# Two layers of cached attention and a token mixer on one core: half of the kv heads stay away from the changes of layer, and their weights' place goes to V

## The chip, the cores and the metric

The kernel runs on one core of one Trainium2 chip. Its time is the device time of one execution in microseconds (us). A profiled execution gives in addition the span from the first to the last instruction and what every engine and every DMA queue did in it.

The engines are named as in the profile: PE multiplies matrices (PEld is its loading of the stationary operand), DVE, ACT and POOL work element by element, and SP here does nothing but issue DMAs, in the order in which the program lists them. An SP instruction that has to wait holds up all loads behind it.

## The reference, cut to what matters

Two identical layers run on `x` of 2 batch rows (b) by 512 channels, one token each. A layer is attention over a cache, then a mixer, each added to its input:

```python
x = x + _A_ref(_layernorm(x), A_k_cache, A_v_cache, A_wq, A_wo)
x = x + _B_ref(_layernorm(x), B_w1, B_b1, B_w2, B_b2)
# the same two lines once more

def _A_ref(x, k_cache, v_cache, wq, wo):       # 32 q heads, 8 kv heads, 32768 cached rows of 128
    q = x @ wq                                  # 4 q heads share one kv head
    p = softmax(q . k * 128 ** -0.5)
    return (p @ v) @ wo

def _B_ref(x, w1, b1, w2, b2):                  # hidden size F = 1792
    h = layernorm(x)
    return gelu(h * w1[f] + b1[f]) summed over f with w2[f], + b2
```

Everything is float32. The caches K and V of one batch row and one kv head are 16.8 MB each, and both layers read the same caches. With 2 rows and 8 heads that is 268 MB for K and 268 MB for V in each layer, and as much again in the second. The weights `wq` and `wo` of one kv head together are 2.1 MB.

## The kernel before, in words

**Units, chunks and slots.** A unit is one (layer, b, h): one kv head of one batch row in one layer. There are 32. A unit's K and its V are cut into 8 chunks (NCH) of 4096 cached rows each: 128 partitions by 16 KB, 2.1 MB. The list `units` gives the order of the units. Slot s handles K chunk s and V chunk s - 10 of that long row of 256 chunks, because V runs one unit and LAG = 2 slots behind K. The main loop (lines 666 to 684) does for each slot: issue the load of K (`load_k`), `k_chunk` on PE, the small steps listed in `pre`, issue the load of V (`load_v`), `v_chunk` on PE, the steps listed in `post`. In slots for which `paired(s)` holds (PAIRED, line 21) two chunks are loaded by one DMA: 32 KB a partition, 4.2 MB. Before the change these are slots 0 to 47 and 212 on.

**PE's work in a slot.** `k_chunk` is 8 matmuls (16 in the records) of scores (line 263); `v_chunk` is 8 matmuls into `acc` (line 353). Per unit there are further: `make_q` (lines 221 and 233) shortly before its first slot, the maximum and the sum of the softmax, `out_1` (line 398, gathers `acc`) in `pre` at the slot in which the next unit's first V chunk is handled, and `out_2` (line 411, times `wo`) in `post` of that slot. After the last unit of a (layer, b) the mixer runs over some ten slots (`mix_1` to `mix_4`, `hidden_tile`, `hidden_out`); its result is needed by `make_q` of that row in the next layer.

**The change of layer.** A layer's first units for row 0 need the mixer's output for row 0. So three units (BRIDGE) of row 1 stand between the last unit (0, 0, h) and the first unit (1, 0, h), and the same holds on the other side for row 1. Layer 1 begins with head 7 (`turned`), which is the last of layer 0, so that V of (0, b, 7) can in part stay in the memory for (1, b, 7).

**The memory.** One tile `mem` of 54,784 floats in each partition (214 KB) holds all of it:

- from 0 to 12,287 the ring: 3 cells of 4096 floats (16 KB) for K and V chunks in turn. Its buffers follow a fixed list, PLACES. In paired slots the ring is 6 cells long, as 3 pairs, and takes part of what comes next, which is then not in use.
- then `kept`, 9728 floats: the parts of V of (0, b, 7) that stay. KEPT says how many of a chunk's 8 quads (a quad is 512 floats a partition, 0.262 MB) stay: 19 of 64 quads. `load_v` loads them in layer 0 and leaves them out in layer 1, for either row.
- then the weights of all 8 heads, 4096 floats each. `load_weights(h)` (line 88) runs once for every head, in `post` six slots ahead of the head's first unit, on SP like all large loads.

A load into a cell waits until PE has read what lay there. With three cells, the load of K chunk s waits for `v_chunk` of slot s - 2, and the load of V in slot s for `k_chunk` of slot s - 1.

**The end.** The last V chunks come in one DMA per piece (PIECES). When the last has come: `v_chunk` multiplies the last 8 row blocks one by one (line 365), `out_1` copies `acc` half on DVE and half on ACT (`halves_copy`, lines 387 and 388) and gathers it by 4 matmuls (line 398), and `last_mixer` multiplies by `wo` with the result spread over all partitions (line 506, 8 matmuls one after the other), takes the statistics (line 514 and on), and does the 14 hidden tiles: the first three by ACT alone (DIRECT, line 546), the others in groups (TAIL_GROUPS) for which DVE does the affine part (line 553) and ACT the gelu (line 557), with PE (line 536) adding them up. Line 563 and the store of line 564 end the program.

Of the kernel before, what the change touches and what calls it, by code (L numbers as in the profile page):

```python
# [8 lines left out]
F32 = mybir.dt.float32  # L9
AF = mybir.ActivationFunctionType  # L10
ALU = mybir.AluOpType
# [6 lines left out]
SUB = 2  # L18
PACK = 4
RING = 3  # L20
PAIRED = ((0, 48), (212, 1 << 30))
LAG = 2
KEPT = {0: 8, 2: 4, 4: 4, 6: 3}
BRIDGE = 3
PIECES = (32, 16, 8, 4, 4)
THIN = 8
QT = 4
DIRECT = 3
TAIL_GROUPS = (3, 3, 4, 1)
EPS = 1e-5  # L30


@with_exitstack
def gqa_mixer_kernel(ctx: ExitStack, tc: tile.TileContext, x, kt, v, wqo, cols, out):

# [35 lines left out]
    nc.scalar.dma_start(xcols, x)  # L73


    W = wqo.shape[2] // 2
    RING0 = 0
    KEPT0 = RING0 + RING * CK
    kept_columns = sum(KEPT.values()) * QT * DH
    order = [HKV - 1] + list(range(HKV - 1))  # L80
    home = {h: KEPT0 + kept_columns + k * 2 * W for k, h in enumerate(order)}
    mem = const.tile([P, KEPT0 + kept_columns + HKV * 2 * W], F32, name="mem")
    kept = mem[:, KEPT0 : KEPT0 + kept_columns]
    wq_sb = [mem[:, home[h] : home[h] + W].rearrange("p (t c) -> p t c", t=DT) for h in range(HKV)]
    wo_sb = [mem[:, home[h] + W : home[h] + 2 * W].rearrange("p (t c) -> p t c", t=R) for h in range(HKV)]

    def load_weights(h):
        nc.sync.dma_start(mem[:, home[h] : home[h] + 2 * W], wqo[h])


    def places(base, k, size):
        return [base + (j % RING) * size for j in range(k, k + RING)]

    PLACES = (
        (PAIRED[0][0], [], places(RING0, 0, 2 * CK)),
        (PAIRED[0][1], [RING0 + j * CK for j in (2, 3, 4)], places(RING0, 0, CK)),
        (PAIRED[1][0], [], places(RING0, 2, 2 * CK)),
    )
    turn = {}

    def buffer(s, size):
        k = max(j for j in range(len(PLACES)) if PLACES[j][0] <= s)
        _, ahead, loop = PLACES[k]
        i = turn.get(k, 0)
        turn[k] = i + 1
        f = ahead[i] if i < len(ahead) else loop[(i - len(ahead)) % len(loop)]
        return mem[:, f : f + size]

    def paired(s):
        return any(a <= s < b for a, b in PAIRED)  # L110

    load_weights(0)
    cols_sb = const.tile([P, 3 * FT + 1], F32, name="cols_sb")
# [15 lines left out]
    nc.vector.tensor_reduce(  # L129
        selg, ident.rearrange("p (g r) -> p r g", g=NG)[:, : R * QT, :], axis=AX.X, op=ALU.add  # L130
    )

    sel1 = selg[:, 0:1].to_broadcast([P, P])
    qpad = [const.tile([P, 64], F32, name=f"qpad{k}") for k in range(2)]
# [13 lines left out]
    def first_input():  # L148
# [19 lines left out]
            xnT[0, b] = const.tile([P, DT], F32, name=f"xnT_0_{b}")  # L168
            nc.vector.tensor_scalar_mul(xnT[0, b], cen[:, b, :], rs[:, b : b + 1])

    heads = list(range(HKV))
    turned = heads[-1:] + heads[:-1]
    lay = {(layer, b): [(layer, b, h) for h in (turned if layer else heads)] for layer in range(LAYERS) for b in range(B)}
    units = (
        lay[0, 0]
        + lay[0, 1][:BRIDGE]
        + lay[1, 0][:-BRIDGE]
        + lay[0, 1][BRIDGE:]
        + lay[1, 0][-BRIDGE:]
        + lay[1, 1]  # L180
    )
    assert len(units) == NU and B == 2

    xT, xnT = {}, {}

    def row_tile():

        return S[HALVES - 1]
# [17 lines left out]
    def unit_of(n):  # L206

        return units[n]

    q_ps = {}  # L210

# [30 lines left out]
    def load_k(s):  # L242
        n, c = divmod(s, NCH)
        layer, b, h = unit_of(n)
        m = 2 if paired(s) else 1
        t = buffer(s, m * CK)
        f0 = (c % 2) * CK
        nc.sync.dma_start(t, kt[b * HKV + h, c // 2, :, f0 : f0 + m * CK])
        for j in range(m):
            k_at[n, c + j] = t[:, j * CK : (j + 1) * CK]  # L250
# [67 lines left out]
    def load_v(s):  # L318
        n, c = divmod(s - NCH - LAG, NCH)
        layer, b, h = unit_of(n)  # L320
        u = b * HKV + h
        m = 2 if paired(s) else 1
        w = QT * DH
        f0 = (c % 2) * CK
        stay = stays(n, c)
        if stay and layer == 0:
            nc.sync.dma_start(kept[:, place[c] : place[c] + stay * w], v[u, c // 2, :, f0 : f0 + stay * w])
        if stay == JT // QT:
            return
        t = buffer(s, m * CK)  # L330
        k0 = stay * QT
        for k in PIECES if s + m == NU * NCH + NCH + LAG else (m * JT - k0,):
            nc.sync.dma_start(t[:, k0 * DH : (k0 + k) * DH], v[u, c // 2, :, f0 + k0 * DH : f0 + (k0 + k) * DH])
            k0 += k
        for j in range(m):
            v_at[n, c + j] = t[:, j * CK : (j + 1) * CK]

    def v_chunk(n, c):
        w = QT * DH
        very_last = n == NU - 1 and c == NCH - 1  # L340
        stay = stays(n, c)
        if stay:
            own = kept[:, place[c] : place[c] + stay * w]
        vc = v_at.pop((n, c), None)
        half, i = divmod(c, PACK)


        a, c2 = divmod(i, PACK // 2)
        quads = JT // QT - (THIN // QT if very_last else 0)
        for q in range(quads):  # L350
            g = q % NG
            col = (c2 * (JT // QT) + q) * 32 + a * R * QT
            nc.tensor.matmul(  # L353
                acc[32 * g : 32 * g + R * QT, :],
                S[half][:, col : col + R * QT],
                (own if q < stay else vc)[:, q * w : (q + 1) * w],
                start=(c == 0 and q < NG),
                stop=(c == NCH - 1 and q >= quads - NG),
            )

        for j in range(quads * QT, JT):
            q, t = divmod(j, QT)
            g = j % NG
            col = (c2 * (JT // QT) + q) * 32 + a * R * QT + t * R
            nc.tensor.matmul(
                acc[32 * g : 32 * g + R, :DH],
                S[half][:, col : col + R],
                vc[:, j * DH : (j + 1) * DH],
                start=False,
                stop=True,  # L370
                skip_group_check=True,
            )
# [8 lines left out]
        rl[n] = work.tile([P, R], F32, name="rl")  # L381
        nc.vector.reciprocal(rl[n], pl[:, :R])  # L382

    def halves_copy(dst, src):

        w = src.shape[1] // 2
        nc.vector.tensor_copy(dst[:, :w], src[:, :w])
        nc.scalar.activation(dst[:, w:], src[:, w:], AF.Copy)

    def out_1(n):  # L390
        asb = row_tile()
        if n == NU - 1:
            halves_copy(asb, acc)
        else:
            nc.vector.tensor_copy(asb, acc)  # L395
        po = pmisc.tile([P, 512], F32, name="misc")
        for t in range(QT):
            nc.tensor.matmul(  # L398
                po[:, :R],
                asb[:, t * DH : (t + 1) * DH],  # L400
                selg[:, t * R : (t + 1) * R],
                start=(t == 0),
                stop=(t == QT - 1),
            )
        oT[n] = work.tile([P, R], F32, name="oT")
        nc.vector.tensor_mul(oT[n], po[:, :R], rl[n])
# [86 lines left out]
    def last_mixer(n):  # L493
# [4 lines left out]
        st = work.tile([P, 2, 6], F32, name="ln_st2", bufs=1)  # L498
        mv = work.tile([P, 2], F32, name="ln_mv")
        rs = work.tile([P, 1], F32, name="ln_rs")  # L500
        space = buffer(NU * NCH, 2 * CK)
        tiles = [space[:, k * D : (k + 1) * D] for k in range(JT2)]
        flat = tiles[JT2 - 1]
        for k in range(2):
            for r in range(R):
                nc.tensor.matmul(  # L506
                    halves[k][:, :w],
                    oT[n][:, r : r + 1].to_broadcast([P, P]),
                    wo_sb[h][:, r, k * w : (k + 1) * w],
                    start=False,  # L510
                    stop=True,
                    skip_group_check=True,
                )
            nc.vector.bn_stats(st[:, k, :], halves[k][:, :w])
        nc.vector.bn_aggr(mv, st)
        deviation(rs, mv)
# [3 lines left out]
        nc.vector.tensor_scalar_mul(scale, w1c, rs)  # L520
        bias = b1c

        res = acc[:, :P]
        for g in range(NG):
            nc.tensor.matmul(
                acc[32 * g : 32 * g + 1, :P],
                ident[:, :1],
                flat[:, g * P : (g + 1) * P],
                start=True,
                stop=False,  # L530
                skip_group_check=True,
            )

        def project(f):
            for g in range(NG):
                nc.tensor.matmul(
                    acc[32 * g : 32 * g + 1, :P],
                    w2c[:, f : f + 1],
                    tiles[f][:, g * P : (g + 1) * P],
                    start=False,  # L540
                    stop=(f == FT - 1),
                    skip_group_check=True,
                )
# [70 lines left out]
    def at(where, slot, f, *a, rank=1):  # L614
        where.setdefault(slot, []).append((rank, f, a))

    for n in range(NU):
        layer, b, h = unit_of(n)
        s0 = n * NCH
        if n:  # L620
            at(post, s0 - 4, make_q, n, 0)
            at(pre, s0 - 3, make_q, n, 1)
            at(post, s0 - 3, make_q, n, 2)
        if n and n < HKV:
            at(post, s0 - 6, load_weights, h)
        at(pre, s0 + NCH, max_1, n)
        at(post, s0 + NCH, max_2, n)
# [3 lines left out]
        at(post, s0 + NCH + LAG + 1, exponentials, n, 1)  # L631
        at(post, s0 + NCH + 4, denominators, n)
        e = s0 + 2 * NCH + LAG
        at(pre, e, out_1, n)
        if n == NU - 1:
            at(post, s0 + NCH + 4, gelu_table)
            at(post, s0 + NCH + 4, last_rows, (layer, b))
# [95 lines left out]
```

## Time and profile before

| | |
|---|---|
| median of 3 runs | 2555.72 us (2555.66 to 2558.36) |
| the profiled execution's own time | 2557.81 us |
| its span, first to last instruction | 2555.9 us |
| PE busy | 1633.2 us, 64% |
| ACT, DVE, POOL busy | 8%, 8%, 0% |
| read from HBM | 1080.58 MB, 423 GB/s over the span |
| TensorE clock granted, mean | 0.809 |

A busy engine here is one with an instruction in work. The DMA rate over a stretch is what the core's 16 DMA engines moved in it. The granted clock takes only the values 1 and 0.5; the same eight matmuls of a chunk take 1.9 us at the one and 3.6 us at the other.

### The profile page before, as it was taken

The page shows a single profiled execution, that of the slowest core. Times are in us where ns is not written, and L with a number is a line of the kernel's source. Part 1 is how long each engine was busy: PE and PEld are TensorE (multiplying, and loading weights), DVE is VectorE, ACT ScalarE, POOL GpSimd, SP SyncE. Part 2 cuts the span into 40 slices and gives each one's busy share as a digit, 9 for nine tenths or more (in the row PEclk, how much of TensorE's full clock was granted, in tenths as well). Part 3 has the DMA queues.
Part 4 walks back from the last instruction along what each step waited for, and adds up shares of the span by engine and source line. Part 5 has one row for each costly group of instructions (what it writes and reads, how often), then busy time and mean ns, then how long its engine had stood idle before and what let it go on. Part 6 is the DMA issues. An engine that isn't in the chain of part 4 may idle for free.

```text
span 2555.9 us, 21591 instructions
## 1 busy us (share of the span) xinstructions
PE 1633.2 (64%) x9700; PEld 412.6 (16%) x9700; DVE 192.3 (8%) x486; ACT 194.6 (8%) x577; POOL 4.9 (0%) x17
## 2 busy tenths in 40 slices
PE   4556566666677667666666665677666766666666
PEld 1111111111111111111111111111111111111112
DVE  1000000000011000000000000001100100000001
ACT  0000000000012000000000000001200200000002
POOL 0000000000000000000000000000000000000000
PEclk8877877787888877787888787878878988788878
DMA  9999999999999999999999999999999999999996
GB/s 417 428 434 429 432 429 431 426 427 422 426 428 428 420 428 415 428 428 428 428 426 428 427 428 423 428 426 428 424 426 429 423 434 430 430 432 432 430 432 264
DMA packets 63174, 1081.99 MB, mean 423 GB/s; under 512 B 7269, under 2 KB 7273, under 8 KB 7914
## 3 DMA queue, kind: packets, MB, share of 16 engines
q1 hardware_dynamic: 62792, 1080.59, 99.3%
q8 instruction: 76, 1.25, 0.2%
q14 instruction: 16, 0.13, 0.0%
q10 hardware_dynamic: 290, 0.03, 0.0%
HBM read 1080.58 MB, written 0.00 MB: 423 GB/s over the span
## 4 chain that ended last, share of the span: by engine, by line
DMA 78%; PE 20%; issue 1%; ACT 0%; DVE 0%; SPq 0%; POOL 0%; ACTq 0%; DVEq 0%
DMA mem<-in_v_dram 40%; DMA mem<-in_kt_dram 39%; PE acc L353 9%; PE scores L263 9%; PE misc L221 1%; PE rows L572 0%; ACT mem L557 0%; PE misc L233 0%; PE bcast L506 0%; PE misc L380 0%; DVE hid L230 0%; ACT S L300 0%; PE misc L398 0%; PE scores L506 0%; ACT mem L546 0%
## 5 line engine op out<-in xcount | busy, mean ns | idle before, releaser
L353 PE MATMUL acc<-mem,S 128*16 128x512 f32 x4092 | 679.8, 799 | 423.9 <-DMA mem<-in_v_dram 421.6
L263 PE MATMUL scores<-mem,qpad 128*32 128x512 f32 x4096 | 656.2, 775 | 426.7 <-DMA mem<-in_kt_dram 426.3
L300 ACT ACTIVATE S<-S,neg 128x128 f32<-128x128 f32 x256 | 130.3, 512 | 2151.9 <-DVE neg L291 1620.2
L263 PEld LDWEIGHTS scores<-mem,qpad 128*32 128x32 f32 x4096 | 143.6, 130 | 859.2 <-issue 536.5
L353 PEld LDWEIGHTS acc<-mem,S 128*16 128x16 f32 x4092 | 124.3, 114 | 903.0 <-DMA mem<-in_v_dram 448.4
L221 PE MATMUL misc<-mem,xnT 128*1 128x512 f32 x256 | 123.4, 613 | 1.6 <-issue 1.6
L273 DVE TENSOR_REDUCE mx<-scores 128x1 f32<-128x512 f32 x64 | 44.3, 692 | 556.5 <-PE scores L263 556.5
L295 DVE STREAM_TRANSPOSE S<-scores 128x512 f32<-128x512 f32 x64 | 45.2, 706 | 178.3 <-PE acc L353 172.9
L233 PE MATMUL misc<-one,hid 1*128 1x1 f32 x256 | 33.8, 249 | 35.4 <-DVE hid L230 35.4
L572 PE MATMUL rows<-hid,cols_sb 128*1 128x512 f32 x84 | 49.4, 673 | 0.6 <-ACT hid L583 0.6
L398 PE MATMUL misc<-selg,S 128*128 128x4 f32 x256 | 38.5, 274 | 15.1 <-DVE S L395 14.5
L300 ACT ACTIVATION_READ_ACCUMULATOR S<-S,neg 128x1 f32 x256 | 47.8, 187 | 0.0
L398 PEld LDWEIGHTS misc<-selg,S 128*128 128x128 f32 x256 | 36.0, 217 | 51.3 <-issue 49.4
L382 DVE RECIPROCAL rl<-misc 128x4 f32<-128x4 f32 x32 | 5.8, 183 | 497.5 <-PE misc L380 497.5
L583 ACT ACTIVATE hid<-bcast,bias,scale 128x512 f32<-128x512 f32 x42 | 32.7, 778 | 129.3 <-PE rows L572 112.2
L233 PEld LDWEIGHTS misc<-one,hid 1*128 1x128 f32 x256 | 31.0, 187 | 65.3 <-DVE hid L230 65.3
L411 PE MATMUL rows<-mem,oT 128*1 128x512 f32 x248 | 38.2, 643 | 0.0
L283 DVE TENSOR_REDUCE m<-misc 1x4 f32<-1x128 f32 x32 | 8.9, 279 | 380.3 <-PE misc L281 380.3
L395 DVE COPY S<-acc 128x512 f32<-128x512 f32 x31 | 21.3, 688 | 202.2 <-PE acc L353 202.2
L221 PEld LDWEIGHTS misc<-mem,xnT 128*1 128x1 f32 x256 | 19.3, 85 | 72.2 <-issue 71.6
L230 DVE COPY hid<-misc 1x512 f32<-1x512 f32 x32 | 21.0, 656 | 52.3 <-PE misc L221 52.0
L291 DVE TENSOR_SCALAR neg<-misc 128x4 f32<-128x4 f32 x32 | 5.2, 162 | 192.0 <-PE misc L289 192.0
(97 smaller groups left out, 207.6 us busy)
## 6 DMA issues: line engine op xcount, KB each, us to landing
mem<-in_kt_dram SPq DMA_DIRECT2D x164, 2048.0 KB, 12.7
mem<-in_v_dram SPq DMA_DIRECT2D x151, 2048.0 KB, 12.5
mem<-in_kt_dram SPq DMA_DIRECT2D x46, 4096.0 KB, 23.7
mem<-in_v_dram SPq DMA_DIRECT2D x45, 4096.0 KB, 23.7
mem<-in_wqo_dram SPq DMA_DIRECT2D x8, 2048.0 KB, 29.7
mem<-in_v_dram SPq DMA_DIRECT2D x13, 1024.0 KB, 12.7
mem<-in_v_dram SPq DMA_DIRECT2D x4, 1280.0 KB, 10.9
mem<-in_v_dram SPq DMA_DIRECT2D x2, 768.0 KB, 14.8
```

The lines of the kernel that those rows point to most:

```text
L221: nc.tensor.matmul(q_ps[n][:1, :], xnT[layer, b][:, d : d + 1], wq_sb[h][:, d, :], start=(d == 0), stop=(d == DT - 1),)
L233: nc.tensor.matmul(pt[:, r : r + 1], q_row[n][:1, r * DH : (r + 1) * DH], one[:1, :], start=True, stop=True)
L263: nc.tensor.matmul(sc_ps[n, half][32 * g : 32 * g + 32, :], q, kc[:, (k * NG + g) * w : (k * NG + g + 1) * w], start=(i == 0 and k == 0), ...
L273: nc.vector.tensor_reduce(mx[n][:, half : half + 1], sc_ps[n, half], axis=AX.X, op=ALU.max)
L295: nc.vector.transpose(S[half], sc_ps[n, half])
L300: nc.scalar.activation(s[:, :, h], s[:, :, h], AF.Exp, bias=neg[n][:, h : h + 1], scale=SCALE, accum_out=lsum[n][:, half, h : h + 1],)
L353: nc.tensor.matmul(acc[32 * g : 32 * g + R * QT, :], S[half][:, col : col + R * QT], (own if q < stay else vc)[:, q * w : (q + 1) * w], st ...
L395: nc.vector.tensor_copy(asb, acc)
L398: nc.tensor.matmul(po[:, :R], asb[:, t * DH : (t + 1) * DH], selg[:, t * R : (t + 1) * R], start=(t == 0), stop=(t == QT - 1),)
L411: nc.tensor.matmul(rows[b][32 * r : 32 * r + 1, :], oT[n][:, r : r + 1], wo_sb[h][:, r, :], start=(units[n] == lay[layer, b][0]), stop=(un ...
L572: nc.tensor.matmul(rows[key[1]][32 * g : 32 * g + 1, :], w2c[:, f : f + 1], hid[key, f], start=(f < NG), stop=(f >= FT - NG),)
L583: nc.scalar.activation(hid[key, f], px[key], AF.Gelu_apprx_tanh, bias=shift[key][:, f : f + 1], scale=slope[key][:, f : f + 1],)
```

## The change

1. **Order of the units.** Heads 0 to 3 ("passing") have their units at the very beginning of layer 0 and late in layer 1, both batch rows of a head next to each other. Heads 4 to 7 (RESIDENT) have theirs around the change of layer; head 7 is still the one whose V stays. The units of index 15 and 20 are now (1, 0, 7) and (1, 1, 7).
2. **Weights.** Heads 4 to 7 keep a place of their own for their weights. Those of heads 0 to 3 are loaded twice, once for each layer, into cells 6, 7, 8 and again 6 of `mem`; between the two, these cells belong to `kept`. There are 12 weight loads in place of 8.
3. **V that stays.** KEPT grows from 19 to 51 of 64 quads: the chunks 0, 1, 3, 4, 6, 7 whole and 3 quads of chunk 2. `kept` now lies in cells 3 to 8 and a part of cell 9. The size of `mem` is as before.
4. **Pairs.** Slots 0 to 93 and 176 on are paired, so 82 slots are left with single chunks in place of 164. The fixed list PLACES is replaced by `buffer`, which takes the cell or the pair that was touched longest ago; a read of `kept` in layer 1 counts as a touch.
5. **The end.** The last row blocks go to `rows[0]` in place of `acc`, so that DVE can add up the four column blocks of `acc` (`add_tiles`) meanwhile; `last_out` replaces `out_1` for the last unit and needs two matmuls in place of four. `last_mixer` multiplies by `wo` into one row per quadrant (four column groups of PE at once), copies the two halves (DVE and ACT) and spreads them by one matmul each. DIRECT goes from 3 to 2, TAIL_GROUPS from (3, 3, 4, 1) to (3, 3, 3, 2, 1). Two small constants, `selh` and `mask`, are made at the start.

```diff
-PAIRED = ((0, 48), (212, 1 << 30))
+PAIRED = ((0, 94), (176, 1 << 30))
 LAG = 2
-KEPT = {0: 8, 2: 4, 4: 4, 6: 3}
+KEPT = {1: 8, 3: 8, 4: 8, 0: 8, 6: 8, 7: 8, 2: 3}
+RESIDENT = (7, 4, 5, 6)
...
-DIRECT = 3
-TAIL_GROUPS = (3, 3, 4, 1)
+DIRECT = 2
+TAIL_GROUPS = (3, 3, 3, 2, 1)
...
-    order = [HKV - 1] + list(range(HKV - 1))
-    home = {h: KEPT0 + kept_columns + k * 2 * W for k, h in enumerate(order)}
-    mem = const.tile([P, KEPT0 + kept_columns + HKV * 2 * W], F32, name="mem")
+    KEPT0 = RING * CK
...
+    passing = [h for h in heads if h not in RESIDENT]
+    home = {h: KEPT0 + kept_columns + k * CK for k, h in enumerate(RESIDENT)}
+    home.update({h: (2 * RING + k % RING) * CK for k, h in enumerate(passing)})
+    mem = const.tile([P, KEPT0 + kept_columns + len(RESIDENT) * CK], F32, name="mem")
...
+    used = [0] * (2 * RING)
+    clock = [0]
+
+    def touch(cells):
+        clock[0] += 1
+        for k in cells:
+            if k < len(used):
+                used[k] = clock[0]
+
+    def buffer(s, m):
+
+        n = 2 * RING if paired(s) or s < PAIRED[0][1] + RING else RING
+        k = min(range(0, n, m), key=lambda k: max(used[k : k + m]))
+        touch(range(k, k + m))
+        return mem[:, k * CK : (k + m) * CK]
...
+    ends = [h for h in RESIDENT[1:]]
+    keeper = HKV - 1
+    units = [(0, b, h) for h in passing for b in range(B)]
+    units += [(0, 0, h) for h in ends + [keeper]]
+    units += [(0, 1, h) for h in ends] + [(1, 0, keeper), (0, 1, keeper)] + [(1, 0, h) for h in ends]
+    units += [(1, 1, keeper), (1, 1, ends[0])]
+    units += [(1, b, h) for h in passing for b in range(B)]
+    units += [(1, 1, h) for h in ends[1:]]
...
+    def add_tiles():
+
+        t = hidden.tile([P, D], F32, name="hid")
+        last_sums[0], last_sums[1] = t[:, :DH], t[:, DH : 2 * DH]
+        nc.vector.tensor_scalar_mul(t[:, :DH], acc[:, :DH], mask[:, 0:1])
+        for k in range(1, QT):
+            nc.vector.scalar_tensor_tensor(
+                t[:, :DH], acc[:, k * DH : (k + 1) * DH], mask[:, k : k + 1], t[:, :DH], op0=ALU.mult, op1=ALU.add
+            )
+
+    def last_out(n):
+
+        nc.vector.tensor_copy(last_sums[1], rows[0][:, :DH])
+        po = pmisc.tile([P, 512], F32, name="misc")
+        for k in range(2):
+            nc.tensor.matmul(po[:, :R], last_sums[k], selh, start=(k == 0), stop=(k == 1))
+        oT[n] = work.tile([P, R], F32, name="oT")
+        nc.vector.tensor_mul(oT[n], po[:, :R], rl[n])
...
         if stay:
+            if layer_of(n):
+                touch(range((KEPT0 + place[c]) // CK, (KEPT0 + place[c] + stay * w - 1) // CK + 1))
...
+        y = row_tile()
+        for k, to in enumerate((rows[b], acc)):
             for r in range(R):
                 nc.tensor.matmul(
-                    halves[k][:, :w],
-                    oT[n][:, r : r + 1].to_broadcast([P, P]),
+                    to[32 * r : 32 * r + 1, :w],
+                    oT[n][:, r : r + 1],
                     wo_sb[h][:, r, k * w : (k + 1) * w],
...
+        nc.vector.tensor_copy(y[:, :w], rows[b][:, :w])
+        nc.scalar.activation(y[:, w:], acc[:, :w], AF.Copy)
+        for k in range(2):
+            nc.tensor.matmul(
+                halves[k][:, :w], sel1, y[:, k * w : (k + 1) * w], start=False, stop=True, skip_group_check=True
+            )
...
-        if n and n < HKV:
+        first = units[n] in ((0, 0, h), (1, 0, h)) if h in passing else units[n] == (0, 0, h)
+        if n and first:
             at(post, s0 - 6, load_weights, h)
...
-        at(pre, e, out_1, n)
+        at(pre, e, out_1 if n < NU - 1 else last_out, n)
```

More of the change, by code (lines that the diff above doesn't have):

```diff
@@ L76, in gqa_mixer_kernel @@
     W = wqo.shape[2] // 2
-    RING0 = 0
-    KEPT0 = RING0 + RING * CK
+    assert CK == 2 * W and HKV == 2 * len(RESIDENT)
+    KEPT0 = RING * CK
     kept_columns = sum(KEPT.values()) * QT * DH
-    order = [HKV - 1] + list(range(HKV - 1))
-    home = {h: KEPT0 + kept_columns + k * 2 * W for k, h in enumerate(order)}
-    mem = const.tile([P, KEPT0 + kept_columns + HKV * 2 * W], F32, name="mem")
+    heads = list(range(HKV))
+    passing = [h for h in heads if h not in RESIDENT]
+    home = {h: KEPT0 + kept_columns + k * CK for k, h in enumerate(RESIDENT)}
@@ L83, in gqa_mixer_kernel @@
+    home.update({h: (2 * RING + k % RING) * CK for k, h in enumerate(passing)})
+    mem = const.tile([P, KEPT0 + kept_columns + len(RESIDENT) * CK], F32, name="mem")
     kept = mem[:, KEPT0 : KEPT0 + kept_columns]
-    wq_sb = [mem[:, home[h] : home[h] + W].rearrange("p (t c) -> p t c", t=DT) for h in range(HKV)]
-    wo_sb = [mem[:, home[h] + W : home[h] + 2 * W].rearrange("p (t c) -> p t c", t=R) for h in range(HKV)]
+    wq_sb = [mem[:, home[h] : home[h] + W].rearrange("p (t c) -> p t c", t=DT) for h in heads]
@@ L87, in load_weights @@
+    wo_sb = [mem[:, home[h] + W : home[h] + 2 * W].rearrange("p (t c) -> p t c", t=R) for h in heads]
     def load_weights(h):
         nc.sync.dma_start(mem[:, home[h] : home[h] + 2 * W], wqo[h])
[L91 to L107, printed above, removed]
     def paired(s):
         return any(a <= s < b for a, b in PAIRED)
+    used = [0] * (2 * RING)
[5 more added lines that the diff above has]
+                used[k] = clock[0]
@@ L131, in gqa_mixer_kernel @@
     )
+    selh = const.tile([P, R], F32, name="selh")
+    nc.vector.tensor_reduce(selh, selg.rearrange("p (t h) -> p h t", h=R), axis=AX.X, op=ALU.add)
+    mask = const.tile([P, QT], F32, name="mask")
+    nc.vector.tensor_reduce(mask, selg.rearrange("p (t h) -> p t h", h=R), axis=AX.X, op=ALU.add)
     sel1 = selg[:, 0:1].to_broadcast([P, P])
@@ L169, in first_input @@
             nc.vector.tensor_scalar_mul(xnT[0, b], cen[:, b, :], rs[:, b : b + 1])
[L171 to L182, printed above, removed]
+    ends = [h for h in RESIDENT[1:]]
+    keeper = HKV - 1
+    assert RESIDENT[0] == keeper and len(ends) == BRIDGE and LAYERS == 2 and B == 2
+    units = [(0, b, h) for h in passing for b in range(B)]
[4 more added lines that the diff above has]
+    units += [(1, 1, h) for h in ends[1:]]
+    assert sorted(units) == sorted((a, b, h) for a in range(LAYERS) for b in range(B) for h in heads)
+    lay = {(a, b): [u for u in units if u[:2] == (a, b)] for a in range(LAYERS) for b in range(B)}
     xT, xnT = {}, {}
@@ L208, in unit_of, with layer_of @@
         return units[n]
+    def layer_of(n):
+        return units[n][0]
     q_ps = {}
@@ L245, in load_k @@
         m = 2 if paired(s) else 1
-        t = buffer(s, m * CK)
+        t = buffer(s, m)
         f0 = (c % 2) * CK
@@ L329, in load_v @@
             return
-        t = buffer(s, m * CK)
+        t = buffer(s, m)
         k0 = stay * QT
@@ L336, in load_v @@
             v_at[n, c + j] = t[:, j * CK : (j + 1) * CK]
+    last_sums = {}
+    def add_tiles():
[13 more added lines that the diff above has]
+        nc.vector.tensor_mul(oT[n], po[:, :R], rl[n])
     def v_chunk(n, c):
@@ L359, in v_chunk @@
             )
+        if very_last:
+            add_tiles()
         for j in range(quads * QT, JT):
@@ L365, in v_chunk @@
             nc.tensor.matmul(
-                acc[32 * g : 32 * g + R, :DH],
+                rows[0][32 * g : 32 * g + R, :DH],
                 S[half][:, col : col + R],
                 vc[:, j * DH : (j + 1) * DH],
-                start=False,
+                start=(j < quads * QT + NG),
                 stop=True,
@@ L382, in denominators @@
         nc.vector.reciprocal(rl[n], pl[:, :R])
[L384 to L388, printed above, removed]
     def out_1(n):
         asb = row_tile()
[L392 to L395, printed above, removed]
+        nc.vector.tensor_copy(asb, acc)
         po = pmisc.tile([P, 512], F32, name="misc")
@@ L500, in last_mixer @@
         rs = work.tile([P, 1], F32, name="ln_rs")
-        space = buffer(NU * NCH, 2 * CK)
+        space = buffer(NU * NCH, 2)
         tiles = [space[:, k * D : (k + 1) * D] for k in range(JT2)]
         flat = tiles[JT2 - 1]
-        for k in range(2):
+        y = row_tile()
+        for k, to in enumerate((rows[b], acc)):
             for r in range(R):
                 nc.tensor.matmul(
-                    halves[k][:, :w],
-                    oT[n][:, r : r + 1].to_broadcast([P, P]),
+                    to[32 * r : 32 * r + 1, :w],
+                    oT[n][:, r : r + 1],
                     wo_sb[h][:, r, k * w : (k + 1) * w],
-                    start=False,
+                    start=True,
                     stop=True,
@@ L521, in last_mixer @@
         bias = b1c
-        res = acc[:, :P]
+        res = rows[0][:, :P]
         for g in range(NG):
             nc.tensor.matmul(
-                acc[32 * g : 32 * g + 1, :P],
+                rows[0][32 * g : 32 * g + 1, :P],
                 ident[:, :1],
@@ L536, in project @@
                 nc.tensor.matmul(
-                    acc[32 * g : 32 * g + 1, :P],
+                    rows[0][32 * g : 32 * g + 1, :P],
                     w2c[:, f : f + 1],
```

## The prediction

> **What bounds the kernel now.** I read the page first: its chain of waits and its DMA rows.
>
> ```profile
> span 2555.9 us, 21591 instructions
> ...
> DMA  9999999999999999999999999999999999999996
> ...
> q1 hardware_dynamic: 62792, 1080.59, 99.3%
> ...
> DMA 78%; PE 20%; issue 1%; ACT 0%; DVE 0%; SPq 0%; POOL 0%; ACTq 0%; DVEq 0%
> ```
>
> The DMA engines are busy in every slice but the last, so the kernel lasts as long as its bytes take, plus the end. Two things can move the time: bytes, and the rate at which they come. For the rate I asked for windows of undisturbed stretches; the last two columns are the share of the DMA engines and GB/s, the one before them is the granted TensorE clock.
>
> ```profile
> 2.00:4.00 2.00, 0.00 (x0) 0.00 (x0) 1.17 (x3) 0.94 (x1) 0.00 (x0) 1.00 0.75 246
> 60.00:440.00 380.00, 225.38 (x1312) 59.17 (x1316) 22.51 (x57) 21.20 (x80) 0.00 (x0) 0.76 1.00 431
> 1060.00:1640.00 580.00, 364.73 (x2166) 85.42 (x2158) 38.96 (x96) 29.89 (x112) 0.00 (x0) 0.81 1.01 427
> 970.00:982.00 12.00, 10.73 (x82) 2.64 (x74) 1.66 (x4) 2.13 (x8) 0.00 (x0) 0.97 0.93 359
> 2250.00:2500.00 250.00, 153.76 (x924) 40.61 (x928) 14.88 (x38) 12.73 (x48) 0.00 (x0) 0.80 1.00 431
> 2535.00:2556.00 21.00, 13.11 (x156) 8.08 (x152) 8.31 (x21) 7.68 (x8) 0.54 (x1) 0.80 0.00 1
> ```
>
> Paired slots (60 to 440, 2250 to 2500) run at 431 GB/s, single ones at 427. The one clear hole is 970 to 982, at 359. The timeline shows what PE did ahead of it: this is the slot in which the first chunk of V that stayed is used.
>
> ```profile
> 961.54 3.64 PE L263 MATMUL scores<-mem,qpad 128*32 128x512 f32 x16 [1.74 <-DMA mem<-in_kt_dram]
> 965.11 1.87 PE L398 MATMUL misc<-selg,S 128*128 128x4 f32 x8
> 966.91 3.62 PE L353 MATMUL acc<-mem,S 128*16 128x512 f32 x16
> 970.30 1.29 PE L411 MATMUL rows<-mem,oT 128*1 128x512 f32 x8
> 971.42 1.89 PE L263 MATMUL scores<-mem,qpad 128*32 128x512 f32 x16
> 973.14 1.89 PE L353 MATMUL acc<-mem,S 128*16 128x512 f32 x16
> ```
>
> At half clock PE needs 9.0 us for K chunk, `out_1` and V chunk; no V load was in flight, so the queue ran dry. It cost 12 x (1 - 359/427) = 1.9 us. From 971 on a chunk takes 1.89 us.
>
> **The change part by part.** Everything is against the profiled execution, 2557.8 us (span 2555.9 and 1.9 around it); it lies 2.1 us above the median of the three runs.
>
> *Bytes.* Thirty-two more quads of 0.262 MB are left out for each row: 2 x 32 x 0.262 = 16.8 MB less, at 427 GB/s -39.3 us. Four more weight loads of 2.1 MB: 8.4 MB, +19.6 us. Net 8.4 MB, **-19.6 us**. Bytes are certain; all of it counts, since nothing else is under DMA's 78% of the chain.
>
> *Pairs.* Slots 48 to 93 and 176 to 211, 82 of 4.19 MB, less the two V chunks that stay, become paired: about 340 MB. At 427 they take 796.3 us, at 431 788.9: **-7.4 us**. Lower bound 0 (the rate belongs to something other than the size), upper 340 x (1/426 - 1/431) = -9.3, from the mean of all single slots, holes and mixers included (426). I take the undisturbed rows.
>
> *The second load of head 0's weights.* In layer 1 it is issued in `post` of slot 170 into cell 6, where chunk 0 of the kept V lies, which `v_chunk` of that very slot reads. SP therefore stands at this load until PE has done slot 170, and the loads of K chunks 171, 172 and the rest stand behind it, though their cells are free: K 171 needs only `k_chunk` of slot 169. When PE starts on K 170, nothing is in flight: there is no V load in slot 170. So DMA idles for K chunk, `out_1`, V chunk: at full clock 1.89 + 1.06 + 1.89 = 4.9 us (1.06: line 398 elsewhere), at half clock the 9.0 us above; and then until bytes flow after an issue. The first load is issued at 0.74 and the two first windows moved 0.59 MB by 4.0 us, 1.4 us' worth, so the flow began 1.9 us after the issue. Together 6.8 to 10.9; between them, as the clock here is 0.81 in the mean, **+9**. Who waits: PE, about 12 us, for K 171. The other weight loads find their cells free for many slots (head 3's second load, slot 218, needs `out_2` of slot 202), and cost only bytes.
>
> *Slots whose V stays (130 to 137, 170 to 177).* For such a unit DMA brings 8 K chunks of 4.9 us and 13 quads, 3.4 MB: 47.3 us. PE at full clock needs 8 x (1.89 + 1.89) = 30.2 and per unit some 8.1 (`make_q` 3.8 + 1.05, `out_1` 1.06, `out_2` 1.05, softmax 1.2): 38.3, which fits under it; at half clock 74, which doesn't. The slot at 961 shows the course: PE begins at half clock, falls behind, and is then granted the full clock. By hand for slot 130: K lands at 0, PE is through with `out_2` at 9.9 and with K 131 at 11.8, and only then can K 133 be issued; in flight is the part chunk of slot 132, which ends at 3 x 4.9 - 1.9 = 12.8 (it is 5 of 8 quads), and K 133 flows from 11.8 + 1.9 = 13.7 on. A hole of 1 us, where the row at 970 had 1.9. I take 2 for the first unit and 1 for the second, where the hole at the weights already let the queue refill: **+3**. Bounds 0, and 12 whole kept chunks x 1.9 = 23.
>
> *The order of units, the mixer of (1, 0) in paired slots, `selh` and `mask`:* 0. The mixers' windows in single slots show 427 as elsewhere; in a paired slot of 19.4 us PE has 7.6 to 14.6 us of chunks. The start's DVE work is covered by the first K load, 18 us; without that cover it would be two reductions of 0.26.
>
> *The end.* From 2535.2 nothing is loaded (1 GB/s), so each step counts.
>
> ```profile
> 2535.65 0.42 DVE L387 COPY S<-acc 128x256 f32<-128x256 f32 x1 [15.37 <-PE acc L365]
> 2536.17 0.38 ACT L388 ACTIVATE S<-acc 128x256 f32<-128x256 f32 x1 [27.85 <-DVE S L387]
> 2537.46 3.68 PE L506 MATMUL bcast<-mem,oT 128*128 128x256 f32 x8 [0.25 <-DVE oT L406]
> 2540.98 1.89 PE L506 MATMUL scores<-mem,oT 128*128 128x256 f32 x8
> 2544.78 2.23 ACT L546 ACTIVATE mem<-mem,cols_sb,scale 128x512 f32<-128x512 f32 x3 [8.23 <-DVE scale L520]
> ```
>
> Line 506 holds the end for 5.4 us. In its place: two rounds of four matmuls side by side (line 411 does 512 columns in 1.05 at full clock, so 256 in 0.53, or 1.05 at half), a copy on ACT of 0.38 (0.8 if it waits for DVE's, as in the second row), a spreading matmul of 0.6 to 0.7 (line 489): 2.0 to 3.6, so -1.8 to -3.4; I take -2.3, nearer to half clock, since line 506 begins there. `add_tiles` starts when `acc` is done (about 2534.9): four DVE steps of 0.3 to 0.4 and a copy of 0.3 end at 2536.4 to 2536.8, then a matmul and the product: about 2537.2 where it is 2537.4 now, -0.2. The gelu groups have as many ACT instructions and as many columns; by the rows (0.74 a direct tile, 1.47 for three, 1.89 for four, 0.61 for one, so about 1.04 for two) 7.5 in place of 7.7: -0.1. **-2.6** (-1.5 to -4).
>
> Sum: -19.6 - 7.4 + 9 + 3 - 2.6 = -17.6. 2557.8 becomes 2540.2; the median, 2555.7, becomes **2538**.
>
> **The rivals.**
>
> *A. Pairs give nothing.* The 4 GB/s could come from the work beside them. For: all the 427 rows have PE work of single slots in them, and nothing else was varied. Against: three long windows agree. Then 2538 + 7.4 = 2545.5. The Trainium skill (DMA: Bandwidth & Descriptors, Rules for kernel authors) asks for 128 partitions and at least 1 MiB in a DMA for the full bandwidth; by that alone both sizes are equal and A would hold. The rows, 427 and 431, disagree a little.
>
> *B. The hole at the weights is hidden*, if K 171 still comes in time: 2538 - 9 = 2529. Against: one queue, in program order.
>
> *C. Each whole kept chunk costs as the one at 970 did:* 23 in place of 3, so 2558, no change. Against: in the second such unit now (1980 to 2060) no such hole is seen.
>
> *D. Slower: PE at half clock sets the pace of the kept slots.* Place: slots 130 to 137 and 170 to 177. PE's 74 us against DMA's 47.3: +26.7; in the second, against 47.3 + 4.9 + 9 = 61: +13. In place of the 3: -17.6 - 3 + 39.7 = +19, 2575. PE's 38.3 us at full clock become 38.3/c at a mean clock c; slower than before by 5.1 needs 2 x 38.3/c - 108 = 25.7, so it decides below a mean clock of 0.57 in these slots. For: 0.5 held for the whole of 961 to 970. Against: a full clock followed, and the window that covers it has 0.97. The Trainium skill (TensorE: Matmul & The Clock Gate, Part 1) says the clock is halved by default and released by some 3.4 us of sustained work, so busy kept slots would be warm and D would fall; the trace agrees in kind, though PE here worked 9 us before its chunks got short.
>
> **How the numbers follow.** Forecast 0.54 (2532 to 2543: hole 6.8 to 10.9, pairs to -9.3, end -1.5 to -4, kept slots 2 to 5), A 0.15, B 0.12, C 0.08, D 0.11. A difference of 0.2%, 5.1 us, is about what a measurement tells from no change. The forecast, A and B are faster by more (0.81), C the same (0.08), D slower (0.11). The range takes in the forecast, A and B: 2527 to 2551.
>
> **What would show it.** HBM read of 1072.2 MB; 12 weight loads; the last load landed at about 2520 us and some 18 us after it. Windows of 431 up to some 910 us and from some 1680 on. SP waiting once for some 7 us at line 88's load, and near it some 9 us without DMA. In the kept units, chunks of 1.9 us. An end in which line 506's 5.4 us are gone. It is wrong if DMA shows holes through all kept slots at half clock, or if the new paired slots stay at 427.

## The result

The changed kernel takes 2539.8 us (median of 4 runs, 2539.0 to 2542.7) where the kernel before takes 2556.5 beside it: a ratio of 0.9936, 95% interval 0.9919 to 0.9953. That is 16.7 us less; 17.6 had been forecast, 2538 us with a range of 2527 to 2551. The profiled execution took 2542.7 us with a span of 2541.0.

From the page of the changed kernel, the lines that answer to those shown of before:

```profile
span 2541.0 us, 21411 instructions
...
DMA  9999999999999999999999999899999999999996
GB/s 413 435 430 429 432 431 431 431 430 433 431 431 430 431 427 428 416 428 421 427 416 426 428 427 427 338 426 429 432 433 430 431 431 430 432 431 430 430 425 283
...
q1 hardware_dynamic: 49688, 1072.19, 98.7%
...
DMA 76%; PE 22%; DVE 1%; issue 0%; ACT 0%; SPq 0%
```

The kernel is still bound by its bytes, now 1072.2 MB, 8.4 less. One slice of the DMA row is not full: the 26th, with 338 GB/s, from 1588 to 1652 us. The windows of the changed kernel (the last columns are granted clock, share of the DMA engines, GB/s) show the new paired stretches (520 to 900, 1700 to 1990) and what the slow slice holds:

```profile
60.00:440.00 380.00, 236.79 (x1386) 62.35 (x1378) 24.12 (x61) 21.18 (x80) 0.00 (x0) 0.77 1.00 431
520.00:900.00 380.00, 234.81 (x1356) 61.76 (x1356) 23.25 (x59) 21.19 (x80) 0.00 (x0) 0.75 1.00 431
1700.00:1990.00 290.00, 181.72 (x1094) 49.71 (x1087) 19.57 (x49) 17.05 (x64) 0.00 (x0) 0.80 1.00 431
1632.00:1634.00 2.00, 2.00 (x12) 0.19 (x4) 0.00 (x0) 0.00 (x0) 0.00 (x0) 0.50 0.66 279
1634.00:1636.00 2.00, 0.35 (x4) 0.00 (x0) 0.69 (x1) 0.00 (x0) 0.00 (x0) 0.50 0.12 49
1636.00:1644.00 8.00, 7.90 (x36) 2.86 (x40) 0.16 (x1) 0.00 (x0) 0.00 (x0) 0.50 0.01 2
1644.00:1646.00 2.00, 2.00 (x16) 0.29 (x8) 0.00 (x0) 0.00 (x0) 0.00 (x0) 0.63 0.00 0
1646.00:1648.00 2.00, 0.21 (x4) 0.00 (x0) 0.00 (x0) 0.00 (x0) 0.00 (x0) 1.00 1.04 254
```

The slots that became paired run at 431 GB/s, as the first ones always did. From 1634 to 1646 us next to nothing is loaded. The timeline of the same stretch names the cause; it is slot 170, the first that uses the V that stayed for (1, 1, 7), with SP's issues between PE's work:

```profile
1636.10 3.64 PE L277 MATMUL scores<-mem,qpad 128*32 128x512 f32 x16 [1.75 <-DMA mem<-in_kt_dram]
1639.67 1.87 PE L428 MATMUL misc<-selg,S 128*128 128x4 f32 x8
1641.47 3.62 PE L390 MATMUL acc<-mem,S 128*16 128x512 f32 x16
1645.15 0.33 SPq L97 DMA_DIRECT2D mem<-in_wqo_dram  x1
1645.53 0.90 SPq L262 DMA_DIRECT2D mem<-in_kt_dram  x2
1657.82 3.64 PE L277 MATMUL scores<-mem,qpad 128*32 128x512 f32 x16 [11.61 <-DMA mem<-in_kt_dram]
```

Head 0's weights are issued the moment PE is through with slot 170, and two K chunks, whose cells had long been free, right behind them. PE then waits 11.6 us for K chunk 171. In SP's own waits this load stands for 19.8 us:

```profile
SPq L97 <- PE acc L390: 19.8, 1, 19.8
```

The end, from the last load on, also from the timeline of the changed kernel:

```profile
2524.01 0.28 DVE L366 COPY hid<-rows 128x128 f32<-128x128 f32 x1
2525.01 0.61 PE L537 MATMUL rows<-mem,oT 128*1 128x256 f32 x8 [0.25 <-DVE oT L371]
2525.44 0.61 PE L537 MATMUL acc<-mem,oT 128*1 128x256 f32 x8
2526.17 0.38 ACT L546 ACTIVATE S<-acc 128x256 f32<-128x256 f32 x1 [30.10 <-DVE S L545]
2527.18 1.06 PE L548 MATMUL scores<-S,selg 128*128 128x256 f32 x2
2530.14 1.52 ACT L583 ACTIVATE mem<-mem,cols_sb,scale 128x512 f32<-128x512 f32 x2 [3.58 <-DVE scale L557]
```

The last load lands at 2522.7 and the span ends 18.2 us later; before it landed at 2535.1 with 20.8 us to go.

### The profile page after: what moved, and what is told of

Read it like the earlier page. It is cut to its first block, busy times and chain, and to the rows that moved or that the text cites. A ratio compares the mean times of both kernels' runs of the same rounds, so it can differ in the third digit from the quotient of the medians.

```text
span 2541.0 us, 21411 instructions
## 1 busy us (share of the span) xinstructions
PE 1619.8 (64%) x9700; PEld 426.5 (17%) x9700; DVE 193.5 (8%) x494; ACT 194.6 (8%) x577; POOL 4.9 (0%) x17
## 4 chain that ended last, share of the span: by engine, by line
DMA 76%; PE 22%; DVE 1%; issue 0%; ACT 0%; SPq 0%
DMA mem<-in_v_dram 40%; DMA mem<-in_kt_dram 36%; PE scores L277 10%; PE acc L390 10%; PE misc L235 2%; PE misc L247 0%; PE rows L609 0%; DVE hid L244 0%; PE misc L428 0%; PE rows L573 0%; PE misc L419 0%; ACT S L314 0%; ACT hid L620 0%; ACT mem L583 0%; ACT mem L594 0%
## 5 line engine op out<-in xcount | busy, mean ns | idle before, releaser
L390 PE MATMUL acc<-mem,S 128*16 128x512 f32 x4092 | 692.7, 824 | 426.0 <-DMA mem<-in_v_dram 421.1
L277 PE MATMUL scores<-mem,qpad 128*32 128x512 f32 x4096 | 638.1, 767 | 404.0 <-DMA mem<-in_kt_dram 393.3
L390 PEld LDWEIGHTS acc<-mem,S 128*16 128x16 f32 x4092 | 137.3, 120 | 914.9 <-issue 537.9
L277 PEld LDWEIGHTS scores<-mem,qpad 128*32 128x32 f32 x4096 | 152.7, 132 | 817.3 <-issue 604.3
## 6 DMA issues: line engine op xcount, KB each, us to landing
mem<-in_kt_dram SPq DMA_DIRECT2D x82, 2048.0 KB, 12.7
```

The costliest lines, as they stand in the source:

```text
L277: nc.tensor.matmul(sc_ps[n, half][32 * g : 32 * g + 32, :], q, kc[:, (k * NG + g) * w : (k * NG + g + 1) * w], start=(i == 0 and k == 0), ...
L390: nc.tensor.matmul(acc[32 * g : 32 * g + R * QT, :], S[half][:, col : col + R * QT], (own if q < stay else vc)[:, q * w : (q + 1) * w], st ...
```

## The experiments

The theory is the sum of the forecast: bytes, paired rate, one hole where SP stands at a load, small losses where V stays, a shorter end. The rivals are A (pairs give nothing), B (no hole), C and D (the slots whose V stays are paced by PE). Losses of a hole are read as its window's length times (1 - its rate / 427).

### The changed kernel again, and the second weight load moved

`after_again` is the changed kernel without an edit:

> The changed kernel once more, as the measure for the three runs beside it. Both theories: 2540 us within 3, one hole of 11 to 14 us without DMA at the second load of head 0's weights (1634 to 1647 us in the trace of the changed kernel).

2539.4 us (2535.9 to 2542.5), ratio to before 0.9927 (0.9912 to 0.9942). From 1630 to 1650 us its DMAs moved 201 GB/s, so 20 x (1 - 201/427) = 10.6 us lost, where the first profile has 138 and 13.5. The hole thus differs from run to run, and below is why.

`w0_slot172` lets K 171, K 172 and the part of V in slot 172 be issued ahead of the weights:

```diff
-            at(post, s0 - 4, make_q, n, 0)
-            at(pre, s0 - 3, make_q, n, 1)
-            at(post, s0 - 3, make_q, n, 2)
+            d = 2 if units[n] == (1, 0, 0) else 0
+            at(post, s0 - 4 + d, make_q, n, 0)
+            at(pre, s0 - 3 + d, make_q, n, 1)
+            at(post, s0 - 3 + d, make_q, n, 2)
...
-            at(post, s0 - 6, load_weights, h)
+            at(post, s0 - 6 + (2 if units[n] == (1, 0, 0) else 0), load_weights, h)
```

> The second load of head 0's weights is issued two slots later (slot 172), behind K chunks 171 and 172 and the part of V in 172; make_q of unit 22 is two slots later too. Theory (SP stands at this load and holds K 171 and all that follows, while nothing is in flight): 12.9 us of loads now lie ahead of it, the hole of 13.3 us shrinks to under 1, so 12 to 13 us less than the changed kernel, about 2527. Rival (the hole comes from PE, which is late in slot 170 and would make K 171 late anyway): the hole stays within 3 us of what it was, 2537 to 2540.

2529.1 us (2528.3 to 2530.9), ratio 0.9888 (0.9874 to 0.9903): 10.3 us less than `after_again`, 2 short of the 12 expected of it. The hole is gone; its window and the timeline around the load, both of `w0_slot172`:

```profile
1630.00:1650.00 20.00, 16.78 (x128) 4.52 (x128) 2.33 (x5) 2.16 (x8) 0.00 (x0) 0.92 1.00 424
```

```profile
1640.27 0.33 SPq L97 DMA_DIRECT2D mem<-in_wqo_dram  x1
1640.89 1.90 PE L277 MATMUL scores<-mem,qpad 128*32 128x512 f32 x16
1642.61 1.90 PE L390 MATMUL acc<-mem,S 128*16 128x512 f32 x16
```

The load still waits for PE's slot 170, but PE goes on to K 171 at once, without the 11.6 us. The rival, that PE itself made K 171 late, falls.

`w0_slot171` is the same edit with 1 in place of the 2 in the last line, so that only K 171 is ahead:

> The same load one slot later (slot 171): only K 171, 4.9 us of loads, is ahead of it. Theory: the load now waits for PE's slot 170 only, which it did before, but K 171 fills 4.9 of the 13.3 us, so a hole of about 8 us and 5 us less than the changed kernel, about 2535. Rival: as in the changed kernel, 2540.

2533.6 us (2530.6 to 2534.6), and 7.1 us lost in the window:

```profile
1630.00:1650.00 20.00, 13.55 (x92) 4.05 (x84) 2.33 (x5) 2.11 (x8) 0.00 (x0) 0.80 0.69 275
```

Nothing ahead loses 10.6 to 13.5, one chunk 7.1, 2.6 chunks 0.1: each chunk of 4.9 us that is already queued covers about its own length.

`warm170` asks what sets the size of the hole. It puts idle matmuls into PE's waits ahead of slot 170:

```diff
+    def warm():
+        p = pmisc.tile([P, 512], F32, name="misc")
+        for _ in range(3):
+            nc.tensor.matmul(p, ident, wq_sb[HKV - 1][:, 0, :], start=True, stop=True)
...
+    at(pre, 169, warm, rank=9)
+    at(post, 169, warm, rank=9)
```

> Six idle matmuls of 512 columns are put into PE's waits of slot 169, so that PE is at full clock when it starts slot 170; nothing else is changed. Theory (the hole is PE's slot 170 at half clock, 9.05 us, and some 4 us between issue, first byte, last byte and landing): slot 170 takes 4.9 to 6 us in place of 9.05 and the hole 9 to 10 in place of 13.3, so 3 to 4 us less, about 2536. Rival (the size of the hole comes from the queue and not from PE's clock): the hole stays at 13, 2540.

Its timeline:

```profile
1632.43 2.31 PE L654 MATMUL misc<-mem,ident 128*128 128x512 f32 x5
1634.93 1.92 PE L277 MATMUL scores<-mem,qpad 128*32 128x512 f32 x16 [0.18 <-DMA mem<-in_kt_dram]
1636.78 1.06 PE L428 MATMUL misc<-selg,S 128*128 128x4 f32 x8
1637.77 1.91 PE L390 MATMUL acc<-mem,S 128*16 128x512 f32 x16
1639.73 0.33 SPq L97 DMA_DIRECT2D mem<-in_wqo_dram  x1
```

PE's slot 170 now takes 4.75 us (1634.93 to 1639.68) in place of 9.0. The windows of the load in the five profiles that have it in this place, `after` (the changed kernel's first profile), `after_again`, `warm170`, and `singles3` and `singles6` of the next section, which leave it as it was:

```profile
1630.00:1650.00 20.00, 13.20 (x64) 3.59 (x64) 0.85 (x2) 0.00 (x0) 0.00 (x0) 0.63 0.37 138
1630.00:1650.00 20.00, 11.67 (x72) 2.62 (x64) 0.85 (x2) 0.00 (x0) 0.00 (x0) 0.67 0.51 201
1630.00:1650.00 20.00, 10.29 (x70) 3.38 (x70) 0.85 (x2) 0.00 (x0) 0.00 (x0) 0.86 0.59 233
1630.00:1650.00 20.00, 12.41 (x72) 3.38 (x64) 0.85 (x2) 0.00 (x0) 0.00 (x0) 0.76 0.42 164
1630.00:1650.00 20.00, 10.81 (x76) 2.65 (x68) 0.85 (x2) 0.00 (x0) 0.00 (x0) 0.84 0.52 202
```

In this order they lose 13.5, 10.6, 9.1, 12.3 and 10.5 us, and PE's slot 170 takes 9.0, 6.2, 4.75, 8.0 and 6.4 us. The differences are 4.5, 4.4, 4.3, 4.3 and 4.1. The hole is PE's slot plus 4.1 to 4.5 us, and the clock that PE happens to have sets the rest. `w0_slot171` fits: PE's slot of 8.0 us, 4.4 more and 4.9 covered make 7.5, and 7.1 were lost. In time this can't be seen: 2539.0 us (2535.2 to 2539.6), the profiled one 2535.2, against a spread of 7 us in `after_again`; 2536 had been expected. What sets the size of the hole is read from the profiles alone.

### The pairs

`singles3` takes the new pairs back:

```diff
-PAIRED = ((0, 94), (176, 1 << 30))
+PAIRED = ((0, 48), (212, 1 << 30))
```

> The changed kernel with pairs only in slots 0 to 47 and from 212 on, as before the change; single chunks in 3 cells elsewhere. Theory (the pairs are worth 427 against 431 GB/s over 340 MB): 7.4 us more than the changed kernel's 2540, about 2547, and 427 in the window of slots 48 to 93. Rival A (pairs give nothing): 2540.

`singles6` does so as well, but lets the single chunks of these slots use all six cells:

```diff
-        n = 2 * RING if paired(s) or s < PAIRED[0][1] + RING else RING
+        n = 2 * RING if paired(s) or s < 94 + RING or s >= 176 else RING
```

> As singles3, but slots 48 to 93 and 176 to 211 have single chunks in all 6 cells, so that up to 5 chunks instead of 2 are in flight. If 16 KB rows themselves are what is slower: 427 GB/s there and about 2547. If it is how much is in flight when PE is late with a cell: 431 and about 2540. Rival A: 2540 here and in singles3.

The windows of what was paired, first of `singles3`, then of `singles6`:

```profile
520.00:900.00 380.00, 229.30 (x1340) 53.41 (x1340) 23.87 (x60) 21.41 (x80) 0.00 (x0) 0.80 1.01 427
1700.00:1990.00 290.00, 182.74 (x1076) 43.08 (x1072) 19.66 (x48) 15.85 (x60) 0.00 (x0) 0.80 1.01 428
```

```profile
520.00:900.00 380.00, 234.54 (x1348) 54.04 (x1340) 24.57 (x61) 21.44 (x80) 0.00 (x0) 0.78 1.01 428
1700.00:1990.00 290.00, 176.38 (x1060) 41.82 (x1060) 18.97 (x47) 14.96 (x56) 0.00 (x0) 0.82 1.01 428
```

At 427 to 428 in place of 431 the slots with single loads are slower, also when six of them have room (over the whole run a 2.1 MB load of K took a median of 21.3 us from issue to landing in `singles6`, 12.7 in `singles3`). So it is not how many are in flight that sets the rate, but the size of one load (or its rows). PE's work beside them is then cut into single chunks too; no run separates that from the size.

The time, however, went up by less than the 7.4 us expected: 2543.2 us (2541.7 to 2545.3) and 2542.6 (2542.3 to 2543.6) against 2539.4 of `after_again`, 3.8 and 3.2, with intervals that overlap (0.9931 to 0.9961 for `singles3`). At 428 GB/s the 340 MB would take 5.5 us more than at 431, at 427 7.4. The changed kernel has, besides, losses that `singles3` has not or has smaller. Its windows

```profile
1680.00:1690.00 10.00, 7.39 (x56) 1.50 (x47) 0.85 (x2) 0.00 (x0) 0.00 (x0) 0.85 0.97 388
2455.00:2465.00 10.00, 9.01 (x74) 2.31 (x70) 0.95 (x3) 0.39 (x2) 0.00 (x0) 0.86 0.93 382
```

lose 0.9 and 1.1 us, where `singles3` has 413 and 434 GB/s. The first lies at the change from single chunks to pairs, the second at the end of the mixer of (1, 0). That the pairs cause them is not shown. `w0_slot171` has the same pairs and neither dip (429 and 446 GB/s from 1670 to 1690, 430 from 2430 to 2490), and in `singles3` too the mixer of (1, 0), slots 241 to 251, falls among pairs. What the hole and the slots whose V stays lose by chance (10.6 to 13.5, and up to 3.3 further below) is as large as the shortfall, so what the pairs are worth in time stays open.

### The bytes

`quads19` goes back to the 19 quads of before and leaves the rest, the second weight loads too:

```diff
-KEPT = {1: 8, 3: 8, 4: 8, 0: 8, 6: 8, 7: 8, 2: 3}
+KEPT = {0: 8, 2: 4, 4: 4, 6: 3}
...
-    kept_columns = sum(KEPT.values()) * QT * DH
+    kept_columns = 51 * QT * DH
```

> The changed kernel with V staying as before the change (19 quads, chunk 0 whole in cell 3), all else the same, the second loads of the weights too. Theory: 16.8 MB more to load, +39.3 us; cell 6 is free when head 0's weights come, so the hole of 11 to 13 us goes, and the kept slots lose 2 us less: 2540 + 39 - 12 - 2 = 2565, slower than before the change. Rival C/D (slots whose V stays are paced by PE, so the bytes left out there bring only part of their price): under 2555.

2568.2 us (2567.8 to 2569.8), 3 above the 2565 expected, ratio to before 1.0044 (1.0029 to 1.0059): the weights twice without more V that stays are a loss. Cell 6 is free in it when head 0's weights come: they are issued at 1643.9 us, and from 1640 to 1670 every 10 us have 426 to 431 GB/s. So it is to be set beside `w0_slot172`, which has no hole either: 2568.2 - 2529.1 = 39.1 us for 16.77 MB, 429 GB/s. The bytes left out bring their whole price. Slots that were paced by PE (C, D) would have given back part of it.

### What the slots lose whose V stays, and the store

The window of 1270 to 1300 us, where the first such unit begins, first in `after_again`, then in `w0_slot171`, which does the same work there; the granted clock differs by chance:

```profile
1270.00:1300.00 30.00, 26.59 (x174) 7.97 (x174) 3.95 (x9) 2.17 (x8) 0.00 (x0) 0.81 0.93 384
```

```profile
1270.00:1300.00 30.00, 24.73 (x190) 7.45 (x190) 3.95 (x9) 2.13 (x8) 0.00 (x0) 1.00 1.01 424
```

At a mean clock of 0.81 they lose 3.0 us, at 1.00 0.2. `best1` has 0.80 and 380 (3.3 us), the first profile of the changed kernel 0.89 and 400 (1.9), `w0_slot172` 0.90 and 418 (0.6). This looks like D's mechanism at a tenth of its size: PE starts these slots at half clock and is then let off. The loss goes with the clock in these profiles; the run that was to force the clock, `best2_warm130` below, doesn't settle it.

`best1` is `w0_slot172` with the mixer's row in a buffer of its own, so that the next scores need not wait for its store:

```diff
-        ysb[key] = row_tile()
+        ysb[key] = row_tile() if layer < LAYERS - 1 else hidden.tile([P, D], F32, name="hid")
```

> w0_slot172 and, besides, the row that the mixer of (1, 0) stores comes from another buffer than the one into which the next scores are turned. In the trace of the changed kernel this turning waits 5.6 us for the store, PE waits for it 7.2 us, and the DMA rate dips by 1.1 to 1.3 us' worth. Theory: 1.1 us less than w0_slot172, about 2528, and no dip there. Rival (the dip is hidden elsewhere): no difference.

2528.8 us (2527.7 to 2529.7), ratio 0.9887 (0.9871 to 0.9904). The dip at the end of the mixer of (1, 0) is gone (426 GB/s from 2440 to 2450, 365 in `w0_slot172`), and the time is the same. One profile of each is thin: `w0_slot171` has no dip either, without this edit. The two profiles differ in the window above by 2.7 us the other way, so a gain of 1.1 is under what these runs can tell.

`best2_warm130` adds the idle matmuls of `warm170` to `best1`, in slot 129, beside `best1` once more:

```diff
+    at(pre, 129, warm, rank=9)
+    at(post, 129, warm, rank=9)
```

> best1 once more, beside the next run: 2529 us within 2; the window of 1270 to 1300 us, in which the first unit with V that stays begins, between 380 and 425 GB/s, by the clock that PE happens to have.

> best1 with six idle matmuls of 512 columns in PE's waits of slot 129, ahead of the first slot whose V stays. Theory (what these slots lose is PE starting them at half clock): granted clock above 0.9 and at least 418 GB/s from 1270 to 1300 us, under 0.7 us lost there; in time 0 to 2.5 us less than best1. Rival C/D (PE's work itself, or the missing V loads, drain the queue): below 410 GB/s there in spite of the clock.

2528.2 us (2527.5 to 2528.6) against 2528.6 (2528.2 to 2529.5): no difference. The clock came out as wanted, 0.98, but the rate at 410, short of the 418; `best1_again`, without the added matmuls, had 0.94 and 420 by chance. The timeline of `best2_warm130`:

```profile
1265.80 4.04 PE L654 MATMUL misc<-mem,ident 128*128 128x512 f32 x6
1269.77 1.91 PE L390 MATMUL acc<-mem,S 128*16 128x512 f32 x16
1271.61 2.84 PE L654 MATMUL misc<-mem,ident 128*128 128x512 f32 x6
1274.38 1.92 PE L277 MATMUL scores<-mem,qpad 128*32 128x512 f32 x16
```

The added matmuls ran at half clock at first, and K of slot 130 (1274.38) starts right behind them without waiting for its load, so PE was late by the work that was to keep it fast. The run is inconclusive on what a full clock alone would give there.

## Why the prediction was right, point by point

The total came out within 2 us, with the bytes, the rate and the end as reckoned. Three terms were off: the hole was 3 us larger than forecast, dips that had been put at 0 cost 2 to 3, and 2.9 us of old holes were not taken off. The first two make the time longer and the third shorter; that the total fits as well as it does is in part luck.

- **Bytes, -19.6.** Right: 39.1 us for twice as many bytes.
- **Pairs, -7.4.** The rate is about right (427 to 428 against 431 with the pairs undone, so 5.5 to 7.4 us); in time only 3.8 and 3.2 were seen. Rival A falls by the windows. The Trainium skill (DMA: Bandwidth & Descriptors, Rules for kernel authors) asks for 128 partitions and at least 1 MiB in a DMA for the full bandwidth. Both sizes meet that, and here the larger is 1% faster. The step "the order of units, the mixer of (1, 0) in paired slots: 0" was off by the 1.1 us of its dip in the changed kernel; the dip of 0.9 at slot 176 and one of 1.2 from 1040 to 1060 us (401 GB/s; 426 before, 427 in `singles3`) I had not priced. What causes these three dips was not found.
- **The second load of head 0's weights, +9.** The mechanism was right to the instruction; the size was 10.6 to 13.5, where "6.8 to 10.9" had been given. PE's part, 4.9 to 9.0, was right. The term that was mis-sized is the 1.9 us "until bytes flow after an issue". By the windows of the changed kernel flow begins 1.7 us after the issue (0.51 MB by 1648, 1.2 us' worth, issue at 1645.15), so that part held. But the queue runs dry before PE starts, too: 0.66 MB moved from 1632 to 1636, 1.5 us' worth, so full flow would have ended at 1633.5, and PE starts on that chunk at 1636.1. I had let the hole begin with PE. The missing 2.6 us make it 4.3 in all; the five profiles above say 4.1 to 4.5. The sign "SP waiting once for some 7 us" came out as 19.8: SP stood at this load from the moment K 170 was issued, and only the part after the queue ran dry costs time.
- **Slots whose V stays, +3.** 1.9 and 3.0 us in the first unit in the two profiles of the changed kernel, none in the second. The sum left out that the holes of before go with it: 1.9 us at 970 (slot 98, which no longer uses V that stayed) and 14 x (1 - 397/427) = 1.0 at 876 (slot 90, now in a pair).
- **The end, -2.6.** 20.8 became 18.2. From the product with `wo` to the second statistics it takes 3.7 us where it took 5.9 (-2.2, forecast -2.3); `last_out` gives nothing (2.2 from the last landing to its result, as before; forecast -0.2), since `add_tiles` ends only 1.3 us after the last load; the gelu tiles 7.7 in place of 8.2 (-0.5, forecast -0.1).

With what was measured: -19.6 - 7.4 + 12 + 2.5 + 3.0 - 2.9 - 2.6 = -15.0, where the hole is the mean of the changed kernel's two profiles, 2.5 that of the kept slots, 3.0 the three new dips (0.9, 1.1 and the mean of 1.2 and 0.8), and 2.9 the holes of before; with 5.5 for the pairs it is -13.1. The two profiled executions took 15.1 and 16.8 us less than that of before (the medians 16.7 and 18.2). Some 1 to 3 us are left that no window names.

Rivals B, C and D fall: the hole is there, the first kept unit loses at most 3.3 us in any profile here, and D's half clock doesn't last. The hole, not the rivals, was where the time was to be had: `best1` and `w0_slot172`, at 0.989 of before, beat the changed kernel.

## What to carry to other kernels

Where one queue issues all loads in order, a load that waits for an engine is paid by every load behind it: place it behind as many free loads as cover the wait (here 2.6 chunks of 4.9 us ahead left 0.1 us lost where the changed kernel lost 10.6 and 13.5). Price such a stop as the engine's work plus both ends of the transfer, the last bytes' way to the waiting engine and the first bytes' way in. And when a forecast adds a hole for the new place, take off the ones that the old place had.

## What the runs showed of the hardware

A queue that runs dry lost 4.1 to 4.5 us beyond the engine's own work, in five profiles. The part after the flow's end is 2.6 and the part ahead of it 1.7, for loads of 2.1 MB issued on SP. The Trainium skill (DMA: Bandwidth & Descriptors, Anatomy of one DMA) puts the fixed cost of one DMA issued from GpSimd at about 2.0 us, most of it after the last byte. No run here issues a large load from there.

Loads of 2.1 MB in 16 KB rows ran at 427 to 428 GB/s with room for three and for six, those of 4.2 MB in 32 KB rows at 431, in every window compared. Whether the row, the total or PE's work beside it makes the difference was not tried.
